# 128-token chunks, slotted attention and one ordered load queue in a linear-attention + MLP kernel on one Trainium2 core

## The chip, the cores and the metric

One core of a Trainium2 chip. The time is the device time of one execution in microseconds (us). The times of the runs below are medians of four executions. Profiles are of one execution each. Engines: PE (TensorE), ACT (ScalarE), DVE (VectorE), POOL (GpSimd), SP (SyncE, which here only issues DMAs).

## The reference

Linear attention with phi(x) = elu(x) + 1 for 8 batches of 8 heads, 576 tokens and head size 64. Its output, 4608 tokens by 512, goes through an MLP of width 2048. Everything is float32 outside and bfloat16 inside.

```python
def phi(x):
    return np.where(x > 0, x, np.exp(x) - 1.0) + 1.0
kv  = np.einsum('bhsd,bhse->bhde', phi(k), v)
z   = np.sum(phi(k), axis=2)
num = np.einsum('bhsd,bhde->bhse', phi(q), kv)
den = np.einsum('bhsd,bhd->bhs', phi(q), z)[..., None] + 1e-06
x   = (num / den).transpose(0, 2, 1, 3).reshape(4608, 512)
h   = x @ w_in                       # 512 -> 2048
out = gelu_tanh(h) @ w_out           # 2048 -> 512
```

A column of ones beside v gives `z` for nothing, so `num` and `den` come from one matmul of 130 columns for two heads.

## The kernel before

Names used throughout: `kv` is the sum over tokens of phi(k) times v; the n matmuls (`nab` in the kernel before, `n_ps` in the changed one) give `num` and `den`; mm1 and mm2 are the two matmuls of the MLP; PSUM is the memory into which PE writes its results, and a DVE or ACT copy out of it is called an evacuation.

Four parts matter: how q, k and v are loaded and made into phi, the attention of two heads, one MLP group of 512 tokens, and how groups are mixed with attention.

```python
CS = 96; NC = S // CS                                  # 6 chunks of 96 tokens
def load_phi(src, b, g, name):
    x_f = pin.tile([128, NC, HH, D], FP32, name=name + "_x")
    for h in range(HH):                                # 256 B runs: one token of one head
        nc.sync.dma_start(out=x_f[0:CS, :, h, :],
            in_=src[b, HH * g + h].rearrange("(c p) d -> p c d", p=CS))
    nc.scalar.activation(e1[0:CS], x_f[0:CS], AF.Exp)  # exp: one ACT table
    # ... min and max-add on DVE

def attention_pair(b, i, qp, kp, vp):                  # 2 heads
    # ... 6 kv matmuls, 6 PE transposes of q + DVE copy, 6 num/den matmuls,
    # ... 2 reciprocals, 2 products, 6 PE transposes of x:
    nc.vector.tensor_copy(XT[:, i, tok0 : tok0 + S], xt_ps)

def mm1_quarter(m0):
    for m in range(m0, m0 + 4):
        h_ps = ps_h.tile([128, TJ], FP32)              # 3 buffers
        # ... 4 matmuls 128x512
        nc.scalar.activation(g[:, m, :], h_ps, AF.Gelu_apprx_tanh)   # other ACT table
# mm2_half: 16 matmuls into ps_o (1 buffer), copy, store

for b in range(B):                                     # 2 MLP units after each pair
    refill(b)
    for g in range(H // HH):
        # ... qp, kp, vp of batch b, head group g
        for i in range(HH // 2):
            attention_pair(b, 2 * g + i, qp, kp, vp)
            drain(2)
```

## Time and profile before

| | before |
|---|---|
| median time (4 runs) | 373.31 us (372.29 to 373.62) |
| span of the profiled run, mean granted clock | 371.7 us, 0.994 |
| MLP matmuls, small PE instructions | 1152, 768 |
| ACT table loads | 46 for exp and gelu |
| DMA packets under 512 B | 114,368 of 121,560 |

The way to read this profile is an account of PE. Count PE's instructions, multiply by their spacing when they run dense, and subtract from the length of a stretch: what is left was lost there. The prediction does so for three stretches. One row of the costliest groups that it does not show is used later (line, engine, what, shapes, count; then busy us, mean ns of one, idle before):

```profile
L188 DVE COPY XT<-xt_ps 128x576 bf16<-128x576 bf16 x32 | 14.6, 455 | 18.3 <-PE xt_ps L179 18.2
```

This is the copy that puts a transposed x into place: 0.455 us each with unit steps on both sides.

### The profile page before, as it was taken

How to read it: one execution, taken by the hardware profiler on the slowest of the kernel's cores; microseconds unless marked ns; L12 is line 12 of the kernel's file. 1: busy time of each engine (PE TensorE's matmuls, PEld its weight loads, DVE VectorE, ACT ScalarE, POOL GpSimd, SP SyncE). 2: the span in 40 equal slices, each digit the busy share in tenths (PEclk: the TensorE clock that was granted, in tenths of full speed). 3: DMA queues.
4: the chain of work that ended last, by engine and by line, in shares of the span. 5: the costliest groups of instructions: out<-in, count | busy, mean ns of one | idle time of the engine just before them, and what ended most of it. 6: DMA issues, size and time to landing. Idle time of an engine off the chain costs nothing.

```text
span 371.7 us, 5098 instructions
## 1 busy us (share of the span) xinstructions
PE 310.7 (84%) x1920; PEld 155.7 (42%) x1920; DVE 180.3 (49%) x299; ACT 208.7 (56%) x304; POOL 32.6 (9%) x54
## 2 busy tenths in 40 slices
PE   0163638998998988799989989999899999999985
PEld 0143213444444544445454544454444554444431
DVE  1656656568557655675477377546731321000000
ACT  0330138845597299974992799499725414613600
POOL 4010300101011010101010120011100000000000
PEclk9999999999899999999999999999999999999999
DMA  9991799955972699046916990697010011011011
GB/s 216 211 301 39 247 268 253 134 138 140 214 115 68 165 198 215 13 131 168 213 34 169 194 196 1 177 212 110 16 69 30 0 58 56 2 56 56 2 56 56
DMA packets 121560, 46.47 MB, mean 125 GB/s; under 512 B 114368, under 2 KB 114368, under 8 KB 121024
## 3 DMA queue, kind: packets, MB, share of 16 engines
q1 hardware_dynamic: 120192, 41.96, 51.9%
q10 hardware_dynamic: 1344, 4.19, 3.3%
q8 instruction: 15, 0.25, 0.3%
q14 instruction: 9, 0.07, 0.1%
HBM read 36.70 MB, written 9.44 MB: 124 GB/s over the span
## 4 chain that ended last, share of the span: by engine, by line
PE 54%; ACT 17%; DMA 8%; issue 8%; DVE 7%; SPq 6%; ACTq 0%; DVEq 0%
PE o_ps L211 27%; PE h_ps L198 20%; ACT g L205 4%; ACT L93 4%; SPq L88 4%; ACT L205 3%; DMA q_x<-in_q_dram 3%; DMA v_f<-in_v_dram 3%; DMA w_stage<-in_moe_w_out_dram 3%; PE nab_ps L147 3%; ACT k_e L93 2%; PE kv_ps L118 2%; SPq L104 2%; ACT q_e L93 1%; PE qt_ps L133 1%
## 5 line engine op out<-in xcount | busy, mean ns | idle before, releaser
L198 PE MATMUL h_ps<-XT,w_in_sb 128*128 128x512 bf16 x576 | 143.8, 390 | 15.7 <-ACT g L205 11.8
L211 PE MATMUL o_ps<-w_out_sb,g 128*128 128x512 bf16 x576 | 135.4, 379 | 5.4 <-ACT g L205 2.4
L205 ACT ACTIVATE g<-h_ps 128x512 bf16<-128x512 f32 x144 | 81.3, 597 | 37.4 <-PE h_ps L198 36.3
L198 PEld LDWEIGHTS <-w_in_sb 128*128 128x128 bf16 x576 | 54.6, 99 | 73.5 <-issue 21.7
L211 PEld LDWEIGHTS <-g 128*128 128x128 bf16 x576 | 54.6, 97 | 68.2 <-issue 6.0
L222 ACT COPY o_sb<-o_ps 128x512 f32<-128x512 f32 x18 | 10.6, 586 | 71.9 <-PE o_ps L211 60.8
L220 DVE COPY o_sb<-o_ps 128x512 f32<-128x512 f32 x18 | 12.4, 690 | 62.6 <-PE o_ps L211 62.5
L93 ACT ACT_TABLE_LOAD x23 | 29.5, 1283 | 9.1 <-DMA q_x<-in_q_dram 8.7
L133 PE MATMUL qt_ps<-ident,q_p 96*128 96x96 bf16 x192 | 14.9, 219 | 22.3 <-DVE q_p L96 20.6
L205 ACT ACT_TABLE_LOAD x23 | 29.5, 1283 | 5.5 <-DVE w_out_sb L80 5.1
L109 POOL MEMSET vp<- 96x1560 bf16 x16 | 24.6, 1540 | 82.8 <-PE kv_ps L118 74.6
L157 DVE RECIPROCAL ra<-nab_ps 96x6 f32<-96x6 f32 x32 | 6.0, 189 | 46.7 <-PE nab_ps L147 46.7
L93 ACT ACTIVATE q_e<-q_x 96x1536 bf16<-96x1536 f32 x16 | 23.7, 1483 | 8.5 <-DMA q_x<-in_q_dram 8.4
L96 DVE SCALAR_TENSOR_TENSOR q_p<-q_x,q_e 96x1536 bf16<-96x1536 f32 x16 | 28.0, 1753 | 0.4
L96 DVE SCALAR_TENSOR_TENSOR k_p<-k_x,k_e 96x1536 bf16<-96x1536 f32 x16 | 27.9, 1746 | 0.3
L147 PE MATMUL nab_ps<-kvbd,qt 128*96 128x130 bf16 x192 | 23.7, 236 | 3.5 <-DVE xa L162 1.5
L147 PEld LDWEIGHTS <-qt 128*96 128x96 bf16 x192 | 17.6, 131 | 19.2 <-DVE xa L162 7.0
L93 ACT ACTIVATE k_e<-k_x 96x1536 bf16<-96x1536 f32 x16 | 23.7, 1482 | 0.1
L118 PE MATMUL kv_ps<-vp,k_p 96*128 96x130 bf16 x192 | 18.2, 231 | 6.5 <-DVE vp L110 6.5
L188 DVE COPY XT<-xt_ps 128x576 bf16<-128x576 bf16 x32 | 14.6, 455 | 18.3 <-PE xt_ps L179 18.2
L133 PEld LDWEIGHTS <-q_p 96*128 96x128 bf16 x192 | 11.7, 104 | 26.3 <-DVE q_p L96 21.9
L128 ACT CAST kvbd<-kv_ps 64x65 bf16<-64x65 f32 x32 | 6.6, 207 | 26.9 <-PE kv_ps L118 26.8
(23 smaller groups left out, 163.4 us busy)
## 6 DMA issues: line engine op xcount, KB each, us to landing
q_x<-in_q_dram SPq DMA_DIRECT2D x64, 144.0 KB, 4.2
k_x<-in_k_dram SPq DMA_DIRECT2D x64, 144.0 KB, 3.7
v_f<-in_v_dram SPq DMA_DIRECT2D x64, 144.0 KB, 4.1
out_dram<-o_sb SPq DMA_DIRECT2D x36, 256.0 KB, 2.1
w_stage<-in_moe_w_in_dram ACTq DMA_DIRECT2D x2, 1024.0 KB, 6.7
w_stage<-in_moe_w_in_dram SPq DMA_DIRECT2D x2, 1024.0 KB, 5.9
w_stage<-in_moe_w_out_dram ACTq DMA_DIRECT2D x2, 1024.0 KB, 9.0
w_stage<-in_moe_w_out_dram SPq DMA_DIRECT2D x2, 1024.0 KB, 7.0
```

Source lines behind the costliest of these rows:

```text
L88: nc.sync.dma_start(out=x_f[0:CS, :, h, :], in_=src[b, HH * g + h].rearrange("(c p) d -> p c d", p=CS),)
L93: nc.scalar.activation(e1[0:CS], x_f[0:CS], AF.Exp)
L96: nc.vector.scalar_tensor_tensor(xp[0:CS], x_f[0:CS], 0.0, e1[0:CS], op0=ALU.max, op1=ALU.add)
L109: nc.gpsimd.memset(vp[0:CS], 1.0)
L118: nc.tensor.matmul(kv_ps, lhsT=kp[0:CS, c, hs, :], rhs=vp[0:CS, c, hs, :], start=(c == 0), stop=(c == NC - 1),)
L133: nc.tensor.matmul(qt_ps[:, CS * c : CS * (c + 1)], lhsT=qp[0:CS, c, hs, :], rhs=ident[0:CS, 0:CS], is_transpose=True, skip_group_check=True,)
L147: nc.tensor.matmul(dst[0:CS, c % 3], lhsT=qt[:, CS * c : CS * (c + 1)], rhs=kvbd, skip_group_check=True,)
L188: nc.vector.tensor_copy(XT[:, i, tok0 : tok0 + S], xt_ps)
L198: nc.tensor.matmul(h_ps, lhsT=w_in_sb[:, c, 128 * m : 128 * (m + 1)], rhs=XT[:, c, tok : tok + TJ], start=(c == 0), stop=(c == KM - 1),)
L205: nc.scalar.activation(g[:, m, :], h_ps, AF.Gelu_apprx_tanh)
L211: nc.tensor.matmul(o_ps, lhsT=g[:, m, 128 * t : 128 * (t + 1)], rhs=w_out_sb[:, m, :], start=(m == 0), stop=(m == MM - 1),)
L220: nc.vector.tensor_copy(o_sb, o_ps)
```

## The change

The intent: fewer small PE instructions, fewer and larger packets, an earlier first MLP group, and attention placed by hand where PE does not wait for it.

- A batch becomes four chunks of 128 rows with token = 4p + c, so four tokens of one head are one run of 1 KB. The last 64 tokens of two batches share one chunk (the "rest").
- Batches 0 to 7 give eight MLP groups of 512 tokens, the rests the ninth.
- The transposes of q and x of batches 2 to 7 and of the rests are DMA transposes of 128 KB, 56 in all.
- All loads, stores and transposes go through SP's one queue, in the order of the program.
- A group has 32 slots (16 of mm1, 16 of mm2). `at(j, slot, fn)` hangs a piece of attention behind one. Exps stand behind the last gelu, so each later batch costs two table loads.
- mm1 and mm2 share five PSUM buffers. 50 dummy matmuls keep PE busy before the first group.

```diff
-    CS = 96
-    NC = S // CS
+    C = 4
+    MAIN = P * C
+    REST = S - MAIN
+    ctx.enter_context(tc.manual_schedule())
     ... 
-        for h in range(HH):
-            nc.sync.dma_start(out=x_f[0:CS, :, h, :],
-                in_=src[b, HH * g + h].rearrange("(c p) d -> p c d", p=CS))
+            eng.dma_start(
+                out=t[:, i * hs : (i + 1) * hs, :],
+                in_=src[b, i * hs : (i + 1) * hs, 0:MAIN, :].rearrange(
+                    "h (p c) d -> p h (c d)", c=C))
     ... start: batch 0 by hand, dummy matmuls between its steps
+        def keep_warm(n):
+            for _ in range(n):
+                nc.tensor.matmul(w_ps, lhsT=warm[:, 0:P], rhs=warm)
     ... later batches
+    def plan_prepare(b, j, s0):
+        def exps():                     # ACT
+            box["k"] = exp_main("k", b)
+            if b % 2 == 0:
+                box["kr"] = phi_rest("kr", b // 2)
+            box["q"] = exp_main("q", b)
+            if b % 2 == 0:
+                box["qr"] = phi_rest("qr", b // 2)
+        at(j, s0, exps)
+        at(j, s0 + 2, lambda: phis("k"))                           # DVE
+        at(j, s0 + 4, lambda: cast_v(b, nc.vector.tensor_copy))    # DVE
+        def qtr():
+            phis("q")
+            for c in range(C):
+                nc.sync.dma_start_transpose(out=qts[b][:, c], in_=...)
+        at(j, s0 + 7, qtr)
+    def plan_attention(b, j, slots):
+        def nab(c):
+            n_ps = ps_a.tile([P, 2, 512], FP32, name="n_ps", tag="a")   # 1 buffer
+            nab_mm(qts[b][:, c], kvbds[b % 4], n_ps)
+            box["x", c] = nab_evac(n_ps)                                # x: 3 buffers
+        def tx(c):
+            nc.sync.dma_start_transpose(
+                out=xts[b][:, :, P * c : P * (c + 1)], in_=...)
+    load_slots = {2: (0, 8), 3: (0, 27), 4: (1, 22)}
+    for b in range(2, B):
+        at(*load_slots.get(b, (b - 3, 15)), lambda b=b: load_batch(b))
+        if b == 2:
+            plan_prepare(b, 0, 31)
+            plan_attention(b, 1, ((8, 9, 10, 11), 11, (15, 17, 19, 21)))
+            at(0, 31, gelu_table)
+        else:
+            plan_prepare(b, b - 2, 15)
+            plan_attention(b, b - 1, ((1, 2, 3, 4), 4, (6, 8, 10, 12)))
+            at(b - 2, 28, gelu_table)
+    for j in range(B + 1):
+        iteration(j)
```

## The prediction

> **What bounds the kernel now.** I read the head of the page first (shares and the 40 slices), then the windows of each engine over three stretches, then the chain of waits, then the DMA queues.
>
> ```profile
> span 371.7 us, 5098 instructions
> PE 310.7 (84%) x1920; PEld 155.7 (42%) x1920; DVE 180.3 (49%) x299; ACT 208.7 (56%) x304; POOL 32.6 (9%) x54
> PE   0163638998998988799989989999899999999985
> DMA  9991799955972699046916990697010011011011
> ```
>
> PE is the busiest engine, but only from the seventh slice on; in the first six DMA is the full row. Busy time overstates pipelined matmuls, so I count instructions times spacing. The spacing comes from the chain of waits (start, length, what), lines of dense runs, and from the timeline for the small matmuls of the attention:
>
> ```profile
> 23.84 1.44 PE h_ps L198 x3
> 312.16 11.38 PE h_ps L198 x52
> 323.55 3.45 PE o_ps L211 x16
> ```
>
> 16 in 3.45 us is 0.2157 us for one 128x512 matmul, so the 1152 of the MLP need 248.5 us whatever the schedule. The first line is the same matmul early on: three took 1.44 us where a dense three takes 0.81 us in the timeline, i.e. half speed.
>
> ```profile
> 163.54 0.33 PE L147 MATMUL nab_ps<-kvbd,qt 128*96 128x130 bf16 x3
> 163.71 0.29 PE L179 MATMUL xt_ps<-ident,xa 96*128 96x96 bf16 x3
> 163.84 0.50 PE L118 MATMUL kv_ps<-vp,k_p 96*128 96x130 bf16 x6
> ```
>
> Start to start, three 130-column matmuls take 0.17 us (0.057 each), three 96-column transposes 0.13 us (0.043 each). The attention's 768 small matmuls are then 384 x 0.057 + 384 x 0.043 = 38 us. Dense PE work is 287 us of 371.7; 85 us are lost. Where, from the windows (length, then PE, PEld, DVE, ACT, POOL busy with counts, clock, DMA share, GB/s):
>
> ```profile
> 0.00:60.00 60.00, 24.43 (x140) 13.68 (x141) 31.56 (x47) 16.99 (x22) 9.63 (x17) 1.00 0.91 219
> 60.00:280.00 220.00, 201.10 (x1344) 103.00 (x1344) 138.04 (x230) 159.99 (x225) 23.01 (x37) 0.99 0.65 136
> 280.00:371.70 91.70, 85.20 (x438) 39.06 (x435) 10.72 (x23) 31.68 (x58) 0.00 (x0) 1.00 0.10 38
> ```
>
> The same windows limited to the tiles h_ps and o_ps give 32, 749 and 373 MLP matmuls. First stretch: 32 x 0.2157 + 108 x 0.05 = 12 us of dense work, 48 lost, DMA busy 0.91. Middle: 162 + 595 x 0.05 = 191 us, 29 lost. End: 80 + 3 = 84, 8 lost, of which 2.3 are three waits of about 0.75 us on the one o_ps buffer and about 3.5 the last copy and store.
>
> ```profile
> DMA packets 121560, 46.47 MB, mean 125 GB/s; under 512 B 114368, under 2 KB 114368, under 8 KB 121024
> q1 hardware_dynamic: 120192, 41.96, 51.9%
> q10 hardware_dynamic: 1344, 4.19, 3.3%
> L93 ACT ACT_TABLE_LOAD x23 | 29.5, 1283 | 9.1 <-DMA q_x<-in_q_dram 8.7
> L205 ACT ACT_TABLE_LOAD x23 | 29.5, 1283 | 5.5 <-DVE w_out_sb L80 5.1
> ```
>
> q, k and v come in 256-byte packets. The weights on q10 took 3.3% of 371.7 x 16 = 196 engine-us for 4.19 MB, 21.4 GB/s per engine, 342 for sixteen. Take the stores (9.44 MB) and the other half of the weights off q1 at that rate (637 us of its 3087): 2450 us stay for 110,592 packets, 22.2 ns each, 185 GB/s. The middle stretch pays for 46 table loads, 59 us of ACT, most of them there, which delay gelus and so the matmuls: the chain there alternates PE with L93 and L205.
>
> **What the Trainium skill says.** (1) "DMA: Bandwidth & Descriptors", section "Why small descriptors are slow (HBM only)": a fixed cost per packet and fixed metadata per operation. The trace agrees: 185 against 342 GB/s. (2) "TensorE: Matmul & The Clock Gate", Part 1: 426.7 ns for N=512 while cold, 215.7 warm, cold after some 3.4 us of idle. The trace agrees (1.44 against 0.81 us for three), though its granted clock says 1.00 there. (3) "ScalarE: Activation LUTs", section "What ACT_TABLE_LOAD costs": about 1283 ns for each load; the page shows 1283. (4) "Advanced Engine Details and Errata", section "X-Bar Transpose (TRN2)": transposing DMAs about as fast as regular ones, 350 to 400 GB/s. No run here shows it yet.
>
> **The change, part by part.**
> PE work. The MLP stays 1152 matmuls, 248.5 us. Chunks of 128 rows: kv is 8 batches x 4 pairs x 5 = 160 matmuls, nab 8 x 16 + 4 x 8 = 160. Only batches 0 and 1 still transpose on PE (2 x 32 = 64). 384 x 0.057 = 22 us in place of 38: 16 saved. All q and x transposes of batches 2 to 7 and of the 64-token rests become DMAs: 6 x 8 + 4 x 2 = 56 of 128 KB, and their PSUM copies leave DVE.
>
> Start-up loads, one queue. Main parts in 1 KB packets, weights in 2 KB, rests in 256 B. A line through 256 B at 22.2 ns and q10's mean of 3.1 KB at 146 ns gives, as an estimate, 55 ns at 1 KB (296 GB/s) and 100 ns at 2 KB (329): 3.55 us for 1 MB of q, k or v, 3.19 us for 1 MB of weights, 0.71 us for half a rest. With 2.5 us to the first bytes: k at 6, q at 9.6, v and rests at 14.6, four w_in parts at 17.8, 21, 24.2 and 27.4, first w_out part at 30.5. Then batch 1 (10.65 + 1.42) at 42.6, w_out to 52.1, q rest 53.6, batch 2 with three rests (14.9) 68.5.
>
> First attention. v at 14.6, its cast on ACT about 1 us, kv at 16, four nab rounds of about 1.4 us (reciprocal 0.19, product 0.69 scaled from 0.55 at 384 columns, the matmuls and handovers), transposes and copies: first xt at about 25. The 34 + 16 dummy matmuls cost nothing, PE waits there anyway, and buy full speed at 25. First MLP group: 64 matmuls of mm1 13.8 us to 39, which the w_in parts do not delay; the first quarter of mm2 to 42.5. Then PE meets kv of batch 1 in its order: after the last gelu ACT loads the exp table (1.28), does k (2048 columns, 1.9 us by 0.83 ns per column from 1483 ns at 1536), k rest and q; DVE then needs 3.5 us for phi of k and 1.6 for the casts. kv at about 48.5, 6 us lost; phi of q to 52; then six slots at about 1.4 us because each nab waits for the evacuation of the one accumulator. Group 0 ends at about 65, DMA (52) close behind it.
>
> Group 1. The exps of batch 2 stand before its gelu table, and one of them needs the last rest of batch 2 (68.5). 0.6 + 1.28 after it gelu can run, PE has filled its five PSUM buffers (20 matmuls) and stops from 69.3 to about 71: 2 us lost.
>
> The rest. From 71: 108 x 0.2157 = 23.3; seven groups 193.3; attention of batches 2 to 7 and rests 248 x 0.057 = 14.1; last copy and store 3.5. That is 305. Per group of about 30 us ACT needs 16 gelus 9.6, exps 3.8, table loads 2.6, copies 1.2 = 17; DVE about 14; DMA 12 for loads, 3.3 for the store, about 4 for transposes: all below PE, and the exps sit behind the last gelu, in mm2, where PE needs no gelu. I add 4 us for small waits: 309 span. The runs before are 1.3 us over the span (373.0 to 371.7): **310 us**.
>
> Sum of the gain of 63: 16 attention on PE, about 15 start-up (48 + lost to about 33), about 25 of the middle's 29, some 4 at the end, the rest rounding.
>
> **Rivals.** (a) The start is bound by DMA all through: if 1 KB packets move at only 216 GB/s, as the first slice does now, the 19.4 MB to the last rest of batch 2 need 90 us instead of 66, group 1 starts its gelus at about 93, and the time is 332. For: the windows' 219 GB/s at 0.91 share. Against: those were 256 B packets, and a slice reached 301. (b) Transposing DMAs are slow or hold up the queue. At 50 GB/s a batch's 1 MB takes 21 us, with loads and stores 36 over a group of 30: DMA becomes the bound, 335 to 345. For: never seen in this trace, one queue for loads, stores and transposes, which waits in order. Against: the skill's figure, and 10 slots or more between issue and use. (c) The gain is larger: DMA runs above 340, group 1 does not stop and nothing small is lost: 300. (d) PE's fixed order lets each late DVE or ACT step stop it, giving back the middle's 29 us: about 325. Against: five shared PSUM buffers and slots placed one group ahead.
>
> **Range and chances.** The floor by this count is 299 (no small waits, faster DMA), (a) with half its effect or (d) with half is 320 to 322. So 298 to 326 for 8 in 10. Slower by 2% needs (a) and (b) in full together with (d): 0.01; within 2%: 0.02; faster: 0.97.
>
> **What would show it.** Right: mm1 of group 0 begins at 23 to 28 us with spacing 0.216; a PE gap near 42 to 50 ended by DVE phi or cast of batch 1; group 0 over at 62 to 70; a short wait on gelu in group 1; from then on groups of 29.4 us with PE near full; 14 table loads (two at the start, two in group 0, two for each of batches 3 to 7) instead of 46; DMA share below 0.8 after 80 us. Wrong: PE gaps of the later groups ended by a DMA (b) or by DVE (d), DMA at 0.95 or over up to 90 us (a), h_ps at 0.43 us spacing early.

## The result, and the profile after

322.21 us median of four runs (320.27 to 323.02), against 373.31 for the kernel before. Ratio 0.8628, 95% interval 0.8599 to 0.8658. A ratio is the mean time of one kernel's fast runs over that of the other's in the same rounds, so not quite the ratio of the two medians. The mean granted clock of the profiled run is 0.969. The prediction of 310, with its range of 298 to 326, holds; it was 12 us low.

The head of the page of the changed kernel, its table loads and its packets:

```profile
span 320.0 us, 4083 instructions
PE 294.1 (92%) x1586; PEld 141.6 (44%) x1586; DVE 128.1 (40%) x239; ACT 160.7 (50%) x215; POOL 9.4 (3%) x22
PE   8969929969969976999999999999999999999993
...
DMA  7999989952115996966599458630245110011022
...
DMA packets 75332, 53.74 MB, mean 168 GB/s; under 512 B 44081, under 2 KB 68657, under 8 KB 75313
...
L148 ACT ACT_TABLE_LOAD x6 | 7.7, 1283 | 0.1
L581 ACT ACT_TABLE_LOAD x6 | 7.7, 1283 | 0.1
```

A slice is 8 us. PE is at work from the first one; in the first three that is in part dummy matmuls. The 2 in the sixth slice is a wait in group 0, the sixes are looked at below, and after the sixteenth slice the row is full. The table loads are these twelve and one of each kind at the start: 14 instead of 46.

The windows, one for each stretch (length, then PE, PEld, DVE, ACT, POOL busy with counts, clock, DMA share, GB/s). They are cut where the first MLP group starts, where groups 0, 1 and 2 end, and at the last matmul:

```profile
0.00:24.02 24.02, 19.52 (x119) 9.53 (x120) 13.91 (x34) 12.64 (x16) 9.37 (x22) 1.00 0.97 335
24.02:64.08 40.06, 33.88 (x196) 17.46 (x196) 20.00 (x35) 22.50 (x25) 0.00 (x0) 0.91 1.05 350
64.08:102.91 38.83, 33.10 (x166) 15.43 (x164) 23.97 (x43) 22.92 (x28) 0.00 (x0) 0.91 0.34 85
102.91:139.93 37.02, 32.33 (x181) 15.49 (x180) 16.81 (x32) 18.04 (x24) 0.00 (x0) 0.95 0.87 249
139.93:315.19 175.26, 175.25 (x929) 83.69 (x927) 52.95 (x97) 84.21 (x122) 0.00 (x0) 1.00 0.40 108
315.19:320.00 4.81, 0.00 (x0) 0.00 (x0) 0.42 (x1) 0.37 (x1) 0.00 (x0) 0.73 0.25 56
```

The same account as in the prediction (0.2157 us for each MLP matmul, 0.057 for each small one): dense work is 248.5 + 384 x 0.057 = 270.4 of 320.0, so 49.6 are lost.

| stretch | length | dense work | lost | predicted lost |
|---|---|---|---|---|
| start, to 24.0 | 24.0 | 3.9 | about 20 | 21 (start at 25) |
| group 0 | 40.1 | 31.5 | 8.6 | 8.5 |
| group 1 | 38.8 | 29.7 | 9.2 | 2, and a share of 4 |
| group 2 | 37.0 | 30.6 | 6.4 | a share of 4 |
| groups 3 to 8 | 175.3 | 174.8 | 0.5 | a share of 4 |
| last copy and store | 4.8 | 0 | 4.8 | 3.5 |

Against the 85 us lost before, the gain of 51.7 in the spans is, by this account, 16 of PE work and about 35.5 of waits. The last 175 us run at PE's pace. What is lost over the prediction lies in groups 1 and 2. PE's timeline between 20 and 125 us, with only the rows whose wait is over 2 us, and the first row of group 0 (start, length, what, count, and in brackets the idle time before and what ended it):

```profile
24.02 13.97 PE L538 MATMUL h_ps<-xt,w_in_sb 128*128 128x512 bf16 x64 [0.67 <-ACT xt L345]
...
47.46 0.59 PE L200 MATMUL kv_ps<-vp,k_p 128*128 128x130 bf16 x4 [6.02 <-DVE vp L185]
...
71.48 5.30 PE L538 MATMUL h_ps<-xt,w_in_sb 128*128 128x512 bf16 x16 [2.91 <-ACT g L545]
...
92.68 0.59 PE L236 MATMUL n_ps<-kvbd,qt 128*128 128x130 bf16 x4 [2.82 <-DVE x L248]
...
122.81 0.66 PE L236 MATMUL n_ps<-kvbd,qtr 128*64 128x130 bf16 x8 [4.69 <-DVE x L248]
```

I call the last three S1 (resumed at 71.48), S2 (92.68) and S3 (122.81). Together they are 10.4 us of idle. The other 5 of the 15.6 us lost in groups 1 and 2 come after the stops: the 16 MLP matmuls after S1 took 5.30 us where a dense 16 take 3.62 in the same timeline, and the granted clock of these windows is 0.91 and 0.95.

What PE waited for is plain; why it was late is another question. S1, by ACT's timeline:

```profile
64.28 0.58 ACT L574 COPY o_sb<-o_ps 128x512 f32<-128x512 f32 x1 [1.14 <-PE o_ps L557]
64.77 1.91 ACT L148 ACTIVATE k_e<-k_x 128x2048 bf16<-128x2048 f32 x1
...
67.10 1.90 ACT L148 ACTIVATE q_e<-q_x 128x2048 bf16<-128x2048 f32 x1
68.90 0.62 ACT L170 ACTIVATE qr_e<-q_r 128x512 bf16<-128x512 f32 x1
69.53 1.28 ACT L581 ACT_TABLE_LOAD   x1
70.83 0.60 ACT L545 ACTIVATE g<-h_ps 128x512 bf16<-128x512 f32 x1
```

From 64.77 on, no row has a wait. Four exps and a table load, 6 us, stand ahead of the first gelu, all placed at the last slot of group 0. The last rest of batch 2 (`q_r`) was not late: its load was issued at 54.0 us and no load of that kind took longer than 10.6 us to land.

S2: PE waits for the one `n_ps` buffer. By DVE's timeline, phi of k of the next batch and an output copy stand ahead of the reciprocal and the product that free it:

```profile
87.87 0.69 DVE L153 TENSOR_SCALAR k_e<-k_e 128x2048 bf16<-128x2048 bf16 x1 [0.72 <-ACT k_e L148]
88.59 2.49 DVE L157 SCALAR_TENSOR_TENSOR k_p<-k_x,k_e 128x512 bf16<-128x512 f32 x4
91.01 0.68 DVE L572 COPY o_sb<-o_ps 128x512 f32<-128x512 f32 x1
91.61 0.19 DVE L246 RECIPROCAL r<-n_ps 128x8 f32<-128x8 f32 x1
91.84 0.69 DVE L248 TENSOR_TENSOR x<-n_ps,r 128x512 bf16<-128x512 f32 x1
```

S3, by DVE's timeline and then by that of SP's queue (start and time the queue needed to issue):

```profile
121.97 0.69 DVE L248 TENSOR_TENSOR x<-n_ps,r 128x512 bf16<-128x512 f32 x1 [5.33 <-DMA xt<-x]
```

```profile
102.83 1.41 SPq L75 DMA_DIRECT2D k_r<-in_k_dram  x2
...
105.58 3.49 SPq L75 DMA_DIRECT2D v_r<-in_v_dram  x2
...
110.90 3.46 SPq L75 DMA_DIRECT2D q_r<-in_q_dram  x2
114.45 0.57 SPq L524 DMA_DIRECT2D out_dram<-o_sb  x1
115.12 1.63 SPq L449 DMA_TRANSPOSE qtr<-qr_p  x1
...
117.49 6.39 SPq L435 DMA_TRANSPOSE xt<-x  x4
```

The first x of batch 3 was ready at 111.5 us, but its transpose was issued at 117.49, behind the whole load of batch 4, two stores and the transpose of the rest's q (`qtr`, itself behind that load). x has three buffers: the product of the rest waited on DVE 5.33 us for a transpose to give one back, and PE waited for DVE. So the page puts S3 down to DVE, and it is the queue of SP.

### The profile page after: what moved, and what is told of

Its sections match the earlier page's. It is cut to its first block, busy times and chain, and to the rows that moved or that the text cites. A ratio compares the mean times of both kernels' runs of the same rounds, so it can differ in the third digit from the quotient of the medians.

```text
span 320.0 us, 4083 instructions
## 1 busy us (share of the span) xinstructions
PE 294.1 (92%) x1586; PEld 141.6 (44%) x1586; DVE 128.1 (40%) x239; ACT 160.7 (50%) x215; POOL 9.4 (3%) x22
## 4 chain that ended last, share of the span: by engine, by line
PE 68%; DVE 2%; DMA 1%; ACT 1%; issue 0%; DVEq 0%
PE o_ps L557 33%; PE h_ps L538 30%; PE n_ps L236 2%; PE kv_ps L200 1%; DMA xt<-x 1%; DVE k_p L157 1%; ACT k_e L148 1%; DVE x L248 0%; PE kv_ps L208 0%; DVE k_e L153 0%; DVE o_sb L572 0%; DVE o_sb L569 0%; ACT o_sb L570 0%; DVE r L246 0%; DVEq L569 0%
## 5 line engine op out<-in xcount | busy, mean ns | idle before, releaser
L538 PE MATMUL h_ps<-xt,w_in_sb 128*128 128x512 bf16 x512 | 122.1, 385 | 3.6 <-ACT g L545 2.9
L572 DVE COPY o_sb<-o_ps 128x512 f32<-128x512 f32 x18 | 12.4, 686 | 64.6 <-PE o_ps L557 64.6
L248 DVE TENSOR_TENSOR x<-n_ps,r 128x512 bf16<-128x512 f32 x36 | 24.9, 691 | 6.5 <-DMA xt<-x 5.3
L157 DVE SCALAR_TENSOR_TENSOR k_p<-k_x,k_e 128x512 bf16<-128x512 f32 (+1 forms) x36 | 20.3, 626 | 0.3
L157 DVE SCALAR_TENSOR_TENSOR q_p<-q_x,q_e 128x512 bf16<-128x512 f32 (+1 forms) x36 | 20.3, 626 | 0.3
L200 PE MATMUL kv_ps<-vp,k_p 128*128 128x130 bf16 x128 | 13.4, 231 | 6.0 <-DVE vp L185 6.0
L236 PE MATMUL n_ps<-kvbd,qt 128*128 128x130 bf16 x128 | 13.0, 224 | 4.8 <-DVE x L248 4.3
L288 PE MATMUL w_ps<-warm 128*128 128x512 bf16 x50 | 14.8, 445 | 1.2 <-DVE warm L120 1.2
L200 PEld LDWEIGHTS <-k_p 128*128 128x128 bf16 x128 | 10.3, 102 | 12.5 <-issue 4.0
L538 PE MATMUL h_ps<-xt_rest,w_in_sb 128*128 128x512 bf16 x64 | 14.0, 379 | 0.0
L148 ACT ACTIVATE k_e<-k_x 128x2048 bf16<-128x2048 f32 x7 | 13.4, 1911 | 0.1
L148 ACT ACTIVATE q_e<-q_x 128x2048 bf16<-128x2048 f32 x7 | 13.3, 1897 | 0.0
```

The lines of the kernel that those rows point to most:

```text
L148: nc.scalar.activation(e, ld[name, b], AF.Exp)
L157: nc.vector.scalar_tensor_tensor(xp[:, c, hs, :], xv[:, c, hs, :], 0.0, ev[:, c, hs, :], op0=ALU.max, op1=ALU.add,)
L200: nc.tensor.matmul(dst, lhsT=kp[:, c, P * i : P * (i + 1)], rhs=vps[b % 2][:, 2 * i : 2 * i + 2, c, :], start=(c == 0), stop=False,)
L236: nc.tensor.matmul(n_ps[rows, i // 2, 2 * E * (i % 2) : 2 * E * (i % 2) + 2 * E], lhsT=qt_c[:, i, rows], rhs=kvbd[:, i, :], skip_group_che ...
L248: nc.vector.tensor_tensor(x, n_v[:, :, :, 0:D], r[:, :, :, None].to_broadcast([P, 2, 4, D]), op=ALU.mult,)
L288: nc.tensor.matmul(w_ps, lhsT=warm[:, 0:P], rhs=warm)
```

## The experiments

A gain or loss against the changed kernel is worked out from the two ratios to the kernel before: the difference from 0.8628, times 373 us. The intervals of the ratios are 0.002 to 0.005 to either side, so about 1 to 2 us. The same start does not take the same time in every profile: in the six runs that leave its code alone, mm1 of group 0 began at 24.02 us (the changed kernel) to 25.18 (phi later), so that about 1 us between two profiles is noise. All runs gave the correct result unless it is said.

The first three take one stop each, the fourth all of them.

**Exps of batch 2 earlier (S1).** Behind slot 25 of group 0, where ACT is idle, instead of 31:

```diff
-        at(j, s0, exps)
+        at(j, s0 - 6 if b == 2 else s0, exps)      # for b == 2 without the rest of q,
+        if b == 2:                                 # which stays at slot 31
+            at(j, s0, lambda: box.__setitem__("qr", phi_rest("qr", 1)))
```

> The exps of batch 2 (k, k rest, q) move from the end of group 0 (slot 31) to slot 25, where ACT idles; only the 0.6 us exp of the q rest stays in front of the gelu table. Theory: the stop of PE in group 1 (68.4 to 71.5 us) is ACT's own queue (6.3 us from the last output copy to the first gelu), not the last load; the stop goes, with the 1.7 us of half-speed matmuls after it: 4.8 us less, span 315. Rival (the step of the prediction): the last rest of batch 2 lands late and holds ACT; the first gelu stays at about 70.8 us and the span at 320.

Measured: 317.52 us (317.28 to 319.1), ratio 0.8523 [0.8488, 0.8557]. That is a gain of 3.9 us, of the 4.8 expected. S1 is gone: the 36 matmuls after group 0 run in 7.93 us without a stop. So S1 was the order on ACT, and neither the DMA nor anything on PE's side. S2 is still there with its 2.82 us.

**Phi of batch 3 later (S2).** Behind the last product of batch 2:

```diff
-        at(j, s0 + 2, lambda: phis("k"))
+        d = 4 if b == 3 else 0
+        at(j, s0 + 2 + d, lambda: phis("k"))       # cast_v and qtr likewise + d
-    load_slots = {2: (0, 8), 3: (0, 27), 4: (1, 22)}
+    load_slots = {2: (0, 8), 3: (0, 27), 4: (1, 26)}
```

> DVE does phi of k, the v cast and phi of q of batch 3 four slots later, after the last product of batch 2. Theory: the PE gap of 2.8 us before the fourth n_ps round (89.9 to 92.7 us) is DVE's order, phi of k standing before the reciprocal; it goes, with 1.2 us at half speed after it: 4 us less, span 316. Rival: DVE has no slack in group 1, so a gap of the same size opens later in group 1 or at the start of group 2 and the span stays at 320.

Measured: 322.1 us (320.96 to 323.4), ratio 0.8628 [0.8581, 0.8675], the ratio of the changed kernel. The gain did not come, although S2 went. The timeline of PE shows where it went, in the row of S3:

```profile
123.34 0.65 PE L236 MATMUL n_ps<-kvbd,qtr 128*64 128x130 bf16 x8 [7.84 <-DVE x L248]
```

S3 grew from 4.69 to 7.84. Counted from the end of S1 in the same trace, PE resumes here after 50.1 us instead of 51.3. So PE reached S3 sooner and waited longer there: what SP's queue has to issue by then is nearly the same. The 2.82 us of S2 lay in the shadow of the gate that comes next; the 1.2 us that are left are within the noise of the start, which was 1.2 us later in this profile.

**Five x buffers (S3).**

```diff
-        x = psm.tile([P, 2, 4, D], BF16, name="x")
+        x = psm.tile([P, 2, 4, D], BF16, name="x", bufs=5)
```

> Five buffers of x (the normalised products) in place of three. Theory: the gap of 4.7 us in group 2 (118.1 to 122.8 us) is DVE waiting for an x buffer whose transposing DMA stands in the SP queue behind the loads of batch 4; with five buffers DVE and PE go on, and 1.7 us at half speed go too: 6.4 us less, span 313.6. Rival: the late transposes themselves are the bound, and PE then waits at the start of group 3 for xt, or for the rest's own transposes; span 318 to 320.

Measured: 319.2 us (317.61 to 319.94), ratio 0.8553 [0.8517, 0.8589], a gain of 2.8 us, less than half of what I expected. S3 in PE's timeline:

```profile
121.85 0.43 PE L236 MATMUL n_ps<-kvbd,qtr 128*64 128x130 bf16 x8 [1.92 <-DMA qtr<-qr_p]
```

DVE no longer waits for x buffers. The wait that remains is for another transpose in the same queue, that of the rest's q. This points to SP's queue; the buffers only decided which of its late items was felt first. That it is the order in the queue, and not the speed of the DMA engines, the next run shows.

**All three together.**

> The three edits together. Theory (three separate stops, each of its own cause): 4.8 + 4.0 + 6.4 = 15.2 us less, span 305 and PE dense from 50 us on. Rival (one shared lack of DVE, ACT or DMA time in groups 1 and 2, which only moves): less than half of it, span 313 or more.

Measured: 307.68 us (307.55 to 308.21), ratio 0.8252 [0.8225, 0.828], a gain of 14.0 us, close to the 15.6 that the account puts into groups 1 and 2. PE's timeline has no wait at all between 58 and 140 us. The single edits gave 3.9, 0.0 and 2.8, together 6.7. Why they add up to more together can be read from SP's queue. S2's edit also moves the load of batch 4 from slot 22 to slot 26, and so behind the transpose of the rest's q (slot 25). In the run with that edit alone:

```profile
98.02 1.19 SPq L450 DMA_TRANSPOSE qtr<-qr_p  x1
99.40 5.53 SPq L405 DMA_TRANSPOSE qt<-q_p  x4
104.99 1.31 SPq L75 DMA_DIRECT2D k_r<-in_k_dram  x2
```

In the changed kernel this `qtr` was issued at 115.12, after the load. It is what PE still waited for with five x buffers, and the x buffers are what it still waited for with S2's edit: each edit alone left the other wait of S3 standing. (The two without S1's edit were not run.) The DMA engines were busy 0.88 of group 2 and 0.96 of group 3 in this run, no less than the 0.87 of the changed kernel, and PE did not wait. So full DMA engines are not what stopped it.

The next four test the parts of the change that the prediction priced.

**Without the dummy matmuls.**

```diff
-            for _ in range(n):
+            for _ in range(0):
```

> The changed kernel without its 50 dummy matmuls. Theory (they cost nothing and buy full speed): mm1 of group 0 starts at about 24 us as before[...]: 2 to 4 us more, span 322 to 324. Rival: the start is set by DMA, ACT and DVE and a slow PE hides: span 320, or less if the dummies delayed the transposes behind them.

Measured: 327.25 us (325.32 to 328.56), ratio 0.8756 [0.8718, 0.8795]: 4.8 us slower. mm1 started at 27.1 us instead of 24.0 (to 25.2 in the runs with the same start), and 61 matmuls of it took 15.81 us (0.259 each) where the changed kernel's 64 took 13.97. So the dummies buy 2 to 3 us in the attention of batch 0, whose small matmuls also run slowly without them (four in 0.61 us instead of 0.41), and some 2.5 in mm1. The prediction had named only the full speed of mm1.

**Small packets again.** Token = 128c + p, four loads instead of one, the store's view to match:

```diff
-                in_=src[b, i * hs : (i + 1) * hs, 0:MAIN, :].rearrange("h (p c) d -> p h (c d)", c=C),
+            for c in range(C):                                   # one load for each chunk
+                in_=src[b, i * hs : (i + 1) * hs, P * c : P * (c + 1), :].rearrange("h p d -> p h d"),
```

> The changed kernel with tokens in chunks of 128 in a row, so q, k and v come in 256-byte packets and in four DMAs each. If loads bound the start (as the prediction had it for larger packets too), 1 MB takes 5.7 us at the 185 GB/s worked out from the kernel before against about 2.7 in the changed kernel's trace: first mm1 8 us later, and group 1 waits for the 9.4 MB of three batches: 10 to 15 us more, span 330 to 335. If the packets only fill waits that exist anyway: under 4 us more.

Measured: 332.86 us (332.74 to 334.28), ratio 0.8919 [0.8896, 0.8943]: 10.9 us slower. The time is as expected, its parts are not: mm1 was expected 8 us later, and the rest of the loss in group 1. The same window of the start in the changed kernel, and then in this one (DMA share and GB/s are the last two columns):

```profile
3.00:13.00 10.00, 9.93 (x47) 4.29 (x46) 7.27 (x21) 6.39 (x7) 3.35 (x9) 1.00 1.10 338
```

```profile
3.00:13.00 10.00, 9.10 (x34) 3.54 (x32) 5.43 (x15) 3.96 (x4) 3.09 (x9) 1.00 1.00 226
```

338 GB/s against 226, with the DMA engines full in both. mm1 of group 0 begins at 29.60 us, 5.6 later. The other 5 us come further on: S3 is 9.33 us instead of 4.69, as more packets and more issues go through the same queue.

**All transposes on PE.** The 56 DMA transposes become PE transposes with a DVE copy, at slots of their own:

```diff
-                nc.sync.dma_start_transpose(out=qts[b][:, c], in_=...)
+            t_q(q_src(b), None, 2 * h, 2, t_ps)                      # nc.tensor.transpose
+            nc.vector.tensor_copy(qts[b][:, 2 * h : 2 * h + 2], t_ps)
```

> The changed kernel with every transpose on PE and a DVE copy, none by DMA. Theory (PE is the bound after 70 us): 224 transposes of 0.056 us are 12.5 us more, and the 6 us of group 2's stop behind the SP queue go: span 324 to 328. Rival (PE is not the bound, the transposing DMAs cost more than they save): span 315 or less.

Measured: 333.43 us (333.38 to 333.76), ratio 0.8929 [0.8911, 0.8947]: 11.2 us slower. PE work grows by 56 x 4 = 224 transposes, at 0.057 us an estimated 12.8 us, about the whole difference. I had expected 4 to 8 us more than the changed kernel, since S3 should go. It goes, but another stop takes its place, with phi of k of the next batch ahead of the product on DVE:

```profile
132.39 0.61 PE L259 MATMUL t_ps<-ident,x 128*128 128x128 bf16 x4 [4.01 <-DVE x L248]
```

So the rival reading, that the DMA transposes cost more than they save because of S3, falls for these slots: without them the kernel is slower, and its PE waits for DVE nearly as long (4.01 us) as it waited for the queue (4.69). Other slots for the PE transposes were not tried.

The next three go back to the kernel before and do one part of the change to it.

**The kernel before without table loads.** Gelu replaced by tanh, which shares a table with exp; the result is wrong.

```diff
-                nc.scalar.activation(g[:, m, :], h_ps, AF.Gelu_apprx_tanh)
+                nc.scalar.activation(g[:, m, :], h_ps, AF.Tanh)
```

> The kernel before with tanh in place of the gelu, a function for which its ACT loads no second table (a wrong result on purpose): no table switches after the first, everything else the same. Theory (the prediction's step on the middle): the 46 loads, 59 us of ACT, are most of the 29 us that PE loses from 60 to 280 us: 20 to 27 us less, span 345 to 352. Rival (the loads sit in ACT's slack; PE loses its time to attention handovers and to cold matmuls at the start): under 8 us less, span 364 or more.

Measured: 361.78 us, ratio 0.9683 [0.9661, 0.9704]: 11.7 us less, half of what the table theory expected. The 46 loads were 59 us of ACT, and taking 45 of them away gives 12 us in all, against the 29 us lost in the middle. The rest of the 29 has other causes; which, these runs do not separate.

**The kernel before with larger runs.** Token = 6p + c in the load, undone in the copy to XT:

```diff
-                in_=src[b, HH * g + h].rearrange("(c p) d -> p c d", p=CS),
+                in_=src[b, HH * g + h].rearrange("(p c) d -> p c d", p=CS),
-        nc.vector.tensor_copy(XT[:, i, tok0 : tok0 + S], xt_ps)
+        nc.vector.tensor_copy(XT[:, i, tok0 : tok0 + S].rearrange("d (p c) -> d c p", c=NC),
+                              xt_ps.rearrange("d (c p) -> d c p", c=NC))
```

> The kernel before with only the token order of its loads changed, six tokens in a row for each partition, so packets of 1.5 KB in place of 256 B (the order is put back in the copy to XT). Theory (the start is bound by small packets): of the 48 us lost in the first 60, 10 to 15 go, span 357 to 362. Rival (the start is bound by the order of loads and waits for buffers, and later loads are hidden): under 4 us less, span 368 or more.

Measured: 386.72 us, ratio 1.0364 [1.0325, 1.0402], slower. The experiment failed in its aim. Its rows for that copy and for the packets:

```profile
L188 DVE COPY XT<-xt_ps 128x576 bf16<-128x576 bf16 x32 | 66.5, 2077 | 15.4 <-PE xt_ps L179 15.3
...
DMA packets 121560, 46.47 MB, mean 121 GB/s; under 512 B 114368, under 2 KB 114368, under 8 KB 121024
```

The packets are the same 114,368. In DRAM a run is now 1.5 KB, but in SBUF the tile is still [chunk, head, 64], so a run there is 256 B, and by the unchanged count the shorter side decides. The changed kernel has 1 KB because it turned the tile too, to [head, (c d)]. And the copy with a 12-byte step on the written side takes 2.08 us instead of 0.455, 52 us more of DVE in all. The run says nothing about larger packets.

**Both edits of the kernel before.** The two diffs above together (wrong).

> Both edits on the kernel before (wrong result on purpose). If the two losses are apart (middle and start), the gains add, span 330 to 342, and most of the change's 52 us is explained by tables and packets alone; if they overlap, less than the larger of the two plus 4 us.

Measured: 388.16 us, ratio 1.0389 [1.0352, 1.0425]. It inherits the flaw of the run before. The 12 us that came from the tables do not come here. My reading, which no run tests: with DVE slowed down, DVE sets the pace and ACT's relief is worth nothing.

Two last runs look for a better kernel.

**Batch 1 before group 0.** All three edits above (the exps of batch 2 behind slot 27 here), and k and q of batch 1 loaded before the third w_in part, exps, phi and cast of batch 1 in the start, weight casts on POOL, and batch 1's kv and num/den matmuls spread over slots 17 to 25 of group 0.

```diff
-    w_st = [load_w(w_in_r, i, "w_st") for i in range(4)]
+    w_st = [load_w(w_in_r, i, "w_st") for i in range(2)]
+    ld["k", 1] = load_main(k, 1, "k_x", nc.sync)
+    ld["q", 1] = load_main(q, 1, "q_x", nc.sync)
+    w_st.append(load_w(w_in_r, 2, "w_st"))
-        for i in range(2):
+        for i in range(4):
             cast_w_in(i, nc.gpsimd.tensor_copy)
...
-        at(j, 19, kv)
+        at(j, 17, kv)
-            at(j, 23 + c, lambda c=c: nab(c))
+            at(j, 19 + 2 * c, lambda c=c: nab(c))
```

> The three edits of the run before, and batch 1 moved ahead: its k and q are loaded before the last two w_in parts, their exps run before the gelu table, phi during the first half of group 0, and GpSimd casts all weights. Theory: the 6.0 us that PE waits for kv of batch 1 (41.4 to 47.5 us), the 2 us at half speed after it and the tight chain of n_ps rounds go: group 0 ends at about 56 us in place of 64, span 306 less 6 to 8 = 298 to 300. Rival (a start bound by DMA): loads in another order only shift the wait to w_in or w_out, mm1 starts or ends later, and the span stays at 304 or more.

Measured: 302.26 us (301.83 to 302.94), ratio 0.8093 [0.8076, 0.8111]. The 6.02 us wait of group 0 is gone, and group 0 ends at 59.2 us instead of 64.1 (56 was expected). mm1 begins later, at 27.53, for two reasons in its trace: the rests of k and v now come whole, and kv of batch 0 waits 1.52 us for the cast of v's rest; and ACT has an exp of batch 1 ahead of the last copies of batch 0, for which PE waits 1.27 us.

**The same, with the start tightened.** The last two copies of batch 0's x on DVE, the second half of v's rest loaded after two w_in parts:

```diff
-                nc.scalar.copy(xt[:, :, P * (c - 1) : P * c], tv[:, 0:NP, :])
+                cp = nc.scalar.copy if c < 3 else nc.vector.tensor_copy
+                cp(xt[:, :, P * (c - 1) : P * c], tv[:, 0:NP, :])
```

> The best version so far with the second half of the v rest loaded two weights later and the last two xt copies of batch 0 on DVE, so that the exp of batch 1 no longer stands before them. Theory: mm1 starts at about 25 us in place of 27.5: 2 to 3 us less, span 297. Rival: the DVE copies delay the n_ps chain by as much: span 299 to 300.

Measured: 300.27 us (300.03 to 301.26), ratio 0.8044 [0.8025, 0.8063]. The start in PE's timeline:

```profile
24.50 4.48 PE L551 MATMUL h_ps<-xt,w_in_sb 128*128 128x512 bf16 x20 [0.52 <-DVE xt L361]
30.00 7.07 PE L551 MATMUL h_ps<-xt,w_in_sb 128*128 128x512 bf16 x31 [1.01 <-ACT g L558]
```

mm1 begins at 24.50 again, but 3 us earlier became 1.8 us of time: PE waits 1.01 us for the first gelus, which stand behind the exps of batch 1 on ACT, and there the exp of q waits for its own load:

```profile
26.13 1.91 ACT L153 ACTIVATE q_e<-q_x 128x2048 bf16<-128x2048 f32 x1 [1.39 <-DMA q_x<-in_q_dram]
```

So here it is ACT's order and a late load together. This is the best version, 0.8044 / 0.8628 = 0.932 of the changed kernel's time.

## Why the prediction was right, and where it was off

**PE work: right.** 384 small instructions at 0.057 us, 16 us saved. Groups 3 to 6 take 29.7 to 30.2 us each and 7 and 8, which have no attention left beside them, 27.6 and 27.8 (predicted 29.4 as a mean with attention), with 0.5 us lost over 175. That no DMA transpose stops them, and that the all-PE version is 11 us slower, bears out the step.

**The start: right in time, wrong in its parts.** mm1 at 24.02 against about 25. The rates were estimated too low: 296 GB/s at 1 KB and 329 at 2 KB. The traces show 338 over 3 to 13 us, mostly 1 KB packets, and, in the same view, 409 over 15 to 20 us, the stretch of the weights. kv of batch 0 began at 13.70 instead of 16; but from there to mm1 it took 10.3 us instead of 9, so that two misses in part cancel. (The prediction also read the DMA row of the kernel before as full in its first six slices; the fourth is a 1, at 39 GB/s.) Rival (a), slow packets all through, falls; the run with 256 B packets shows what it would have cost, 10.9 us.

**Group 0: right.** 8.6 us lost against 8.5, a wait of 6.02 ended by the cast of v of batch 1, and the end at 64.08 against 65.

**Group 1's wait: the right time for the wrong reason.** PE resumed at 71.48 where the prediction had 71 and gave "one of them needs the last rest of batch 2 (68.5)". The load was there by 64.6 at the latest; ACT had 6 us of exps and table load in a row. Moving the exps alone removed the stop, with no load moved, so the cause is shown. A right number does not check its derivation.

**The mis-sized term: "I add 4 us for small waits".** With the 2 us of group 1 that is 6 us for everything after group 0; it measured about 16 (9.2 + 6.4 + 0.5). This is the step that made 310 of 322. The prediction checked each engine's sum over a group (ACT 17, DVE 14, DMA about 19 of 30 us) and found all below PE. For ACT and DVE the sums held, for DMA on average only (see below). What stopped PE was the order within each in-order engine: exps ahead of gelus on ACT, phi ahead of an evacuation on DVE, loads ahead of transposes on SP. These are rival (d) on ACT and DVE, and rival (b)'s "one queue" on SP. (d) was set aside with the five PSUM buffers and the slots placed one group ahead, (b) with the skill's figure and the ten slots between issue and use; neither looks at what stands ahead of an item in its own queue. Rival (d)'s figure does not follow either: giving back what the prediction had gained in the middle, 25 us or more, makes 335 and not 325. What happened is (d) and (b)'s queue in part; that "half" of (d), put at 320 to 322, meets the measured 322 is luck. Where the order is loose (groups 3 to 8) they cost nothing; in groups 1 and 2 the pieces of two batches lie close together. The run with all three mended, 307.68, is about what the prediction said.

**The end: 4.8 against 3.5.** The last tile's copy is split over DVE and ACT, but the halves ran one after the other (315.27 to 315.69 on DVE, then from 315.73 on ACT). The sum of the misses is 10 for the waits and 1.3 for the end, less 1 for the earlier start: 10.3, and the span is 320.0 against 309.

**Table loads: 14 as predicted, but their worth was taken as larger than shown.** The prediction put about 25 of the middle's 29 us to the change, and read the loads as its main cause. In the kernel before they are worth 12. In the changed kernel the middle gained about 13 (29 lost before; 16 now).

**DMA share below 0.8 after 80 us: right on average, wrong in group 2,** where it is 0.87 over 37 us, 32 us of DMA against the 19 of the sum: the loads of batches 4 and 5 both fall into it. By the run with all three edits (0.88 there, no wait) this alone does not stop PE.

**Still open.** What makes up the other 17 us lost in the middle of the kernel before; and how much larger packets alone would give there, since that experiment did not change the packets.

## What to carry to other kernels

When every engine's sum is below the bound, go through the order of each in-order engine, the DMA queue too, and ask of each item that PE waits for: what stands ahead of it, and for how long? A stop costs PE its length and often 1 to 2 us more in slow matmuls after it, and removing one may give nothing while a later gate in another queue stands: here single edits gave 3.9, 0.0 and 2.8 us, and together 14.0. Before counting on larger packets, look at the contiguous run on both sides of the transfer.

## What the Trainium skill lacked or had wrong

- "DMA: Bandwidth & Descriptors", section "Measured (HBM→SBUF, 128 partitions, SWDGE, issued from GpSimd)": its table goes by size of transfer and for GpSimd's queue. No page has rates measured on this chip, by packets of 256 B to 2 KB, for loads that SyncE issues. The runs show 226 GB/s with 256 B (3 to 13 us of the start), 338 with mostly 1 KB in the same window, and 409 with 2 KB (15 to 20 us).
- "Advanced Engine Details and Errata", section "X-Bar Transpose (TRN2)": "TRN2 transpose DMAs are as fast as regular DMAs". One of 128 KB lands in 2.4 us (median), a store of 128 KB in 2.3, so it agrees. The section does not give the time to issue one of this size: 1.2 us of the queue (median of 24), against 0.6 for many loads of 1 MB. One queue can thus issue some 107 GB/s of these transposes (an estimate, 128 KB by 1.22 us), far below the section's 350 to 400.
- "VectorE: DVE Perf Modes" has its plainest mode for any step, and no page puts a figure on what a wide step costs a VectorE copy. A bf16 copy of 128x576 out of PSUM took 0.455 us with unit steps and 2.08 us with a 12-byte step on the written side, 4.6 times as long; losing the two-at-a-time mode would explain a factor of two at most.
- "TensorE: Matmul & The Clock Gate", Part 1, gives an idle window of about 3.4 us that runs freely. The runs agree that it varies: after a gap of 2.82 us at S2, four small matmuls took 0.59 us in the changed kernel and 0.40 in the run with earlier exps, and the 40 of mm2 behind them 10.01 and 8.79. So a gap of 2.8 us, shorter than that window, may already cost the slow stretch.
- No page says of the granted clock that a profile shows (as apart from the events of the clock gate) that it can read 1.00 while the matmuls run at half speed, as in parts of the first 60 us of the kernel before (three in 1.44 us instead of 0.81).
